# Moving two of three value loads to a second DMA queue in a decode-attention kernel

## The chip, the cores and the metric

One core of a Trainium2 chip. The metric is the device time of one execution in microseconds, the median of the runs. All runs told here are fast (none is over 1.5% above the fastest run of its kernel). Transfers are issued by an engine's sequencer into a queue (0.33 us an issue on SyncE); SyncE has one and ScalarE has one (q1 and q10 in the traces below), and the packets of both run on the core's 16 DMA engines. A load has landed when its completion is counted. A turn is three blocks, one for each buffer.

## The reference, cut to what matters

One query token attends to a cache of 65,536 keys and values in 16 heads of 256, beside a small dense branch:

```python
q = (xn @ wq).reshape(1, 1, 16, 256).transpose(0, 2, 1, 3)
scores = einsum("bhqd,bhkd->bhqk", q, k_cache) * 256 ** -0.5
o = einsum("bhqk,bhkd->bhqd", softmax(scores), v_cache)
out = x + (o.transpose(...).reshape(1, 1, 4096) @ wo) * silu(silu(xn @ w1) @ w2)
```

The cache is 1.07 GB and each byte is used once.

## The kernel before

The cache is cut into 64 blocks; a block's keys are one load of 128 partitions x 64 KB (8.389 MB), and so are its values. There are three buffers. In each, keys come in; VectorE forms the products with the query and sums them for 19 columns of 32, ScalarE sums the other 13; the values come into the same buffer; TensorE multiplies them with the exponentials; then the buffer takes the keys of three blocks later. SyncE issues everything:

```python
    def load_k(i, s, h=None):
        if h is not None:
            take(sp, h)                  # TensorE is past half of the buffer's values
        take(sp, vf[s])                  # TensorE is done with the buffer
        sp.dma_start(out=R[s][:, :], in_=block(Kd, i)).then_inc(kl[s], 16)
        ...
    def load_v(i, s):
        take(sp, kf[s])                  # VectorE's last copy of the block: keys are used up
        sp.dma_start(out=R[s][:, :], in_=block(Vd, i)).then_inc(vl[s], 16)
    ...
    def dve_block(s, between=None):      # VectorE, cut
        take(dve, qr)
        dve.tensor_copy(out=qcur[:, :], in_=ps_q).then_inc(sd, 1)
        take(dve, kl[s], 16)             # ALL of the block's keys must have landed
        ...                              # 4 x (one long multiply, 19 multiply-and-sum)
        take(dve, pf, 4)                 # ScalarE's last sums
        dve.tensor_copy(out=S2[...], in_=S[...]).then_inc(kf[s], 1)
        dve.reduce_max(out=rmax[:, :], in_=S[...], axis=AX.X).then_inc(rm, 1)
    ...
    def act_block(i, s):                 # ScalarE
        for k in range(NSTEP):
            if k == NSTEP // 2:
                act_keep(i - 2)
            act_sums(s, k)
        act_softmax(i, s)                # waits for the maximum, then the exponentials
    ...
        with nc.Fori(2 * NR, LAST - 2, NR, engines={ET.SP}, ...) as i:
            for s in range(NR):
                load_k(i + s, s, vh[s])
                load_v(i + s - 1, (s - 1) % NR)
```

The kernel waits until a load's counter has risen by 16, and the trace has 16 four-byte completion records to a load (112 for the seven loads in a window of 130 us). I take them as one for each engine (the records do not name theirs); so a load has landed when the slowest engine is done (in one block of before the last completion record came at 1222.0 and the landing was counted at 1222.46).

## Time and profile before

| | before |
|---|---|
| time, median of 3 runs (range) | 2520.83 us (2520.53 to 2522.59) |
| share of the span in which SyncE's DMA queue was busy | 99.7% |
| rate in steady slices | 433 GB/s |
| VectorE busy | 89% |
| VectorE's wait for keys | 190.1 us, 61 times |

The share of the queue says what bounds the kernel; VectorE's wait for keys says that the next in line has room. The lines themselves are shown, and read, in the prediction.

### The profile page before, as it was taken

Reading aid. Unit: us, or ns where it says so; the run is one execution under the profiler, and the core shown is the slowest. Engines: PE = TensorE matmul, PEld = TensorE weight load, DVE = VectorE, ACT = ScalarE, POOL = GpSimd, SP = SyncE. Lnnn points to the kernel's source line nnn. Section 1 sums busy time; section 2 is a strip of 40 time slices with the busy share of each in tenths; the row PEclk is TensorE's granted clock in tenths of the full one; section 3 lists DMA queues with packets and bytes.
Section 4 is the critical chain, followed back from the end, with each engine's and each line's share of the span. In section 5 each row is a group of like instructions: output and inputs, shape, how many; then the busy total and the mean of one; then the engine's idle time right before and its main releaser. Section 6 shows DMA issues by size and latency. Waiting matters only on the chain. (4 is left out here: it accounts for less than half of the span.)

```text
span 2518.0 us, 29489 instructions
## 1 busy us (share of the span) xinstructions
PE 1147.2 (46%) x4738; PEld 437.0 (17%) x4738; DVE 2233.4 (89%) x10277; ACT 1446.0 (57%) x6996; POOL 1.9 (0%) x14
## 2 busy tenths in 40 slices
PE   3253543534535435345354353453543534535457
PEld 1121211211112112112111121111111211211122
DVE  6979889889898898898998988989989889889897
ACT  4656556556565565565655655655556556556564
POOL 0000000000000000000000000000000000000000
PEclk7676766767667677677676776776776767767679
DMA  9999999999999999999999999999999999999998
GB/s 422 426 440 420 432 435 431 435 433 433 433 433 433 433 433 433 433 433 433 433 433 433 433 433 433 433 433 433 433 433 434 434 433 433 434 435 436 433 427 357
DMA packets 23316, 1084.47 MB, mean 431 GB/s; under 512 B 2434, under 2 KB 4612, under 8 KB 4996
## 3 DMA queue, kind: packets, MB, share of 16 engines
q1 hardware_dynamic: 23298, 1084.30, 99.7%
q8 instruction: 4, 0.07, 0.0%
q14 instruction: 12, 0.10, 0.0%
q10 hardware_dynamic: 2, 0.00, 0.0%
HBM read 1084.29 MB, written 0.00 MB: 431 GB/s over the span
## 5 line engine op out<-in xcount | busy, mean ns | idle before, releaser
L283 ACT ACTIVATE R<-R 128x256 bf16<-128x256 bf16 x3328 | 1330.8, 401 | 747.5 <-ACTq L159 747.5
L261 DVE CUSTOM_DVE_ANT_0 R<-R,qcur 128x256 bf16<-128x256 bf16 x4864 | 1700.3, 418 | 0.0
L330 PE MATMUL bank<-R,PV 128*2 128x512 bf16 x4096 | 1027.1, 417 | 29.6 <-DMA R<-in_A_v_cache_dram 11.5
L250 DVE TENSOR_TENSOR R<-R,qcur 128x3328 bf16<-128x3328 bf16 x256 | 482.8, 1886 | 190.1 <-DVEq L159 190.0
L283 ACT ACTIVATION_READ_ACCUMULATOR R<-R 128x1 f32 x3328 | 620.9, 187 | 0.0
L342 PE MATMUL bank<-ident,rmax 128*1 128x128 bf16 x65 | 17.1, 263 | 1076.8 <-PEq L159 1076.8
L330 PEld LDWEIGHTS bank<-R,PV 128*2 128x2 bf16 x4096 | 366.0, 90 | 662.4 <-issue 212.9
L261 DVE DVE_READ_ACCUMULATOR2_ANT S<- 128x1 f32 x4864 | 387.1, 80 | 0.0
L342 PEld LDWEIGHTS bank<-ident,rmax 128*1 128x1 bf16 x65 | 5.2, 79 | 1081.1 <-issue 1081.0
L359 PE MATMUL bank<-eye,O 2*128 2x2 f32 x264 | 40.0, 252 | 232.2 <-PEq L159 232.2
L296 ACT ACTIVATE hist<-bank 128x1 f32 (+1 forms) x65 | 11.1, 171 | 199.5 <-ACTq L159 199.5
L359 PEld LDWEIGHTS bank<-eye,O 2*128 2x128 f32 x264 | 36.2, 206 | 249.5 <-issue 249.5
L224 DVE TENSOR_REDUCE gmax<-bank 1x1 bf16<-1x128 f32 x65 | 18.3, 281 | 37.2 <-DVEq L159 37.2
L309 ACT COPY O<-bank 2x512 f32<-2x512 f32 x67 | 37.4, 559 | 21.6 <-ACTq L159 21.6
L317 ACT COPY hist<-bank 128x2 f32 (+1 forms) x66 | 10.5, 159 | 59.9 <-ACTq L159 59.9
L241 DVE CAST qcur<-bank 128x256 bf16<-128x256 f32 x64 | 27.2, 424 | 19.0 <-DVEq L159 19.0
L298 ACT ACTIVATE PV<-S,hist 128x128 bf16<-128x128 f32 (+1 forms) x65 | 26.0, 400 | 13.4 <-ACTq L159 13.1
L373 PE MATMUL bank<-q,ident 8*128 (+1 forms) x63 | 24.3, 386 | 7.7 <-issue 1.3
L234 DVE COPY S<-S 128x128 f32<-128x128 f32 (+1 forms) x65 | 14.7, 226 | 10.4 <-DVEq L159 1.1
L235 DVE TENSOR_REDUCE rmax<-S 128x1 bf16<-128x128 f32 (+1 forms) x65 | 18.1, 279 | 0.0
L348 PE MATMUL bank<-gmax,ones_row 1*128 1x1 bf16 x65 | 10.3, 159 | 4.5 <-PEq L159 0.6
L298 ACT ACTIVATION_READ_ACCUMULATOR PV<-S,hist (+1 forms) x65 | 12.1, 186 | 0.0
(68 smaller groups left out, 90.6 us busy)
## 6 DMA issues: line engine op xcount, KB each, us to landing
R<-in_A_k_cache_dram SPq DMA_DIRECT2D x7, 4096.0 KB, 27.3
R<-in_A_v_cache_dram SPq DMA_DIRECT2D x6, 2048.0 KB, 22.4
R<-in_A_k_cache_dram SPq DMA_DIRECT2D x2, 2048.0 KB, 20.1
R<-in_A_wq_dram SPq DMA_DIRECT2D x1, 3072.0 KB, 12.8
R<-in_A_v_cache_dram SPq DMA_DIRECT2D x3, 1024.0 KB, 25.0
R<-in_A_wo_dram SPq DMA_DIRECT2D x2, 1120.0 KB, 21.8
R<-in_B_w_dram SPq DMA_DIRECT2D x1, 1568.0 KB, 25.7
R<-in_B_w_dram SPq DMA_DIRECT2D x1, 1344.0 KB, 5.8
```

What stands on the lines that cost most here:

```text
L224: dve.reduce_max(out=gmax[0:1, :], in_=ps_m[0:1, :], axis=AX.X).then_inc(gm, 1)
L235: dve.reduce_max(out=rmax[:, :], in_=S[:, c0:c1], axis=AX.X).then_inc(rm, 1)
L241: dve.tensor_copy(out=qcur[:, :], in_=ps_q).then_inc(sd, 1)
L250: m = dve.tensor_tensor(out=pair, in0=pair, in1=qcur[:, None, :].to_broadcast([P, NA, Dh]), op=ALU.mult,)
L261: ins = dve.tensor_tensor_reduce(out=Kv[:, c, :], in0=Kv[:, c, :], in1=qcur[:, :], scale=1.0, scalar=0.0, op0=ALU.mult, op1=ALU.add, accum ...
L283: ins = act.activation(out=prod, in_=prod, func=ACT.Identity, accum_out=S[:, c : c + 1],)
L298: act.activation(out=PV[s][:, c0:c1], in_=S2[:, c0:c1], func=ACT.Exp, bias=col(0, 1), scale=scale, accum_out=col(1, 2),).then_inc(pv, 1)
L309: act.copy(out=O[:, :], in_=po).then_inc(oc, 1)
L330: ins = pe.matmul(po, lhsT=PV[t][:, c : c + 2], rhs=R[s][:, c * Dh : (c + 2) * Dh], start=(start and c == k0), stop=(stop and c == k1 - 2),)
L342: pe.matmul(ps_m[0:1, :], lhsT=rmax[:, 0:1], rhs=ident[:, :], start=True, stop=True).then_inc(tm, 1)
L359: ins = pe.matmul(ps_t2[:, 2 * a : 2 * a + 2], lhsT=Ov[:, j, a, :], rhs=eye2[:, j, :], start=(j == 0), stop=(j == 1), is_transpose=True,)
L373: pe.matmul(ps_q, lhsT=ident[0:HP, at(j)].to_broadcast([HP, P]), rhs=q8[:, o : o + Dh] if isinstance(o, int) else q8[:, bass.ds(o, Dh)], s ...
```

## The change

Its intent: take value loads out of SyncE's single stream of waits, so that one of them is issued as soon as ScalarE, which stands at the right place anyway, sees its condition met. The third buffer's value loads stay in SyncE's queue.

```diff
-    def load_v(i, s):
-        take(sp, kf[s])
-        sp.dma_start(out=R[s][:, :], in_=block(Vd, i)).then_inc(vl[s], 16)
+    def load_v(i, s, g=sp):
+        take(g, kf[s])
+        g.dma_start(out=R[s][:, :], in_=block(Vd, i)).then_inc(vl[s], 16)
@@ act_block
             act_sums(s, k)
+        if s < NR - 1:
+            load_v(i, s, act)
         act_softmax(i, s)
@@ SyncE's stream
         load_k(2, 2)
-        load_v(0, 0)
-        load_v(1, 1)
...
             load_k(NR + s, s, vh[s])
-            load_v(NR + s - 1, s - 1)
...
                 load_k(i + s, s, vh[s])
-                load_v(i + s - 1, (s - 1) % NR)
+                if s == 0:
+                    load_v(i - 1, NR - 1)
```

## The prediction

> **What bounds the kernel now.** I read the page's slices and queue table first, then the issues by line, then the timeline of SyncE, VectorE and TensorE in the middle of the run, and last the row that waits longest on the busiest engine.
>
> ```profile
> span 2518.0 us, 29489 instructions
> PE 1147.2 (46%) x4738; PEld 437.0 (17%) x4738; DVE 2233.4 (89%) x10277; ACT 1446.0 (57%) x6996; POOL 1.9 (0%) x14
> DMA  9999999999999999999999999999999999999998
> GB/s 422 426 440 420 432 435 431 435 433 433 433 433 433 433 433 433 433 433 433 433 433 433 433 433 433 433 433 433 433 433 434 434 433 433 434 435 436 433 427 357
> q1 hardware_dynamic: 23298, 1084.30, 99.7%
> L250 DVE TENSOR_TENSOR R<-R,qcur 128x3328 bf16<-128x3328 bf16 x256 | 482.8, 1886 | 190.1 <-DVEq L159 190.0
> ```
>
> The reader is to see that one DMA queue (SyncE's) is busy for 99.7% of the span and moves 433 GB/s slice after slice, while the busiest engine, VectorE, is at 89% and still waits 190 us. That wait is in 61 places, 3.1 us each: once in a block, for the block's keys. The transfers bound the kernel, and the VectorE is next. The chain of waits reaches back only to the last 7 us and says nothing of the loop.
>
> One block of the loop, from the timelines (start, duration, engine):
>
> ```profile
> 1218.00 0.33 SPq L207 DMA_DIRECT2D R<-in_A_v_cache_dram  x1
> 1236.26 0.33 SPq L201 DMA_DIRECT2D R<-in_A_k_cache_dram  x1
> 1256.70 0.33 SPq L207 DMA_DIRECT2D R<-in_A_v_cache_dram  x1
> 1274.39 0.33 SPq L201 DMA_DIRECT2D R<-in_A_k_cache_dram  x1
> 1295.50 0.33 SPq L207 DMA_DIRECT2D R<-in_A_v_cache_dram  x1
> 1312.52 0.33 SPq L201 DMA_DIRECT2D R<-in_A_k_cache_dram  x1
> ```
> ```profile
> 1217.61 0.23 DVE L234 COPY S<-S 128x128 f32<-128x128 f32 x1
> ...
> 1219.33 16.64 PE L330 MATMUL bank<-R,PV 128*2 128x512 bf16 x64
> 1219.40 0.17 ACT L296 ACTIVATE hist<-bank 128x1 f32 x1 [3.08 <-ACTq L159]
> ...
> 1222.60 1.89 DVE L250 TENSOR_TENSOR R<-R,qcur 128x3328 bf16<-128x3328 bf16 x1 [3.07 <-DVEq L159]
> ```
> ```profile
> R<-in_A_v_cache_dram SPq DMA_DIRECT2D x62, 23.8
> R<-in_A_k_cache_dram SPq DMA_DIRECT2D x60, 25.5
> ```
>
> A value load is issued 0.16 us after VectorE's copy ends (1217.84). A key load is issued when TensorE has used up a buffer: 17.0 to 18.3 us after the value load, 17.7 on average. Value issues stand 38.70 and 38.80 us apart; from 250.32 to 2417.77 they are 56 blocks, so a block takes 38.70 us and one load of 8.389 MB takes half, 19.35 us (433.5 GB/s). VectorE needs 34.1 us from the landing of its keys to the next value issue (1222.60 to 1256.70), then about 1.5 us for maximum and query before it could start again: 35.6 us, hence its 3.1 us of waiting. The value load of 1218.00 lands at 1241.8, but TensorE starts on it only after the next block's maximum, at 1258.03: values have 16 us to spare, keys none.
>
> [...]
> - [...] The trace of before can't show two queues side by side, but shows how little there is to save: 0.33 us an issue, on an engine that does nothing else.
> - [...]
> - [...]
> - [...] The trace: the 1344 KB load at the start lands 5.8 us after issue, of which 3.2 us is data at 433 GB/s, so 2.6 us; I use 2.6.
>
> **The change part by part.**
> 1. *Where the issue stands.* For two blocks of three, waiting for VectorE's copy and issuing the value load move to ScalarE. VectorE's copy itself waits for ScalarE's last sums, so ScalarE is there in time. It then waits anyway: 3.08 us idle before the bias copy that opens its exponentials, which started 1.56 us after the copy ended (1217.84 to 1219.40). The wake-up and issue, 0.16 + 0.33 us [...], fit in these 1.56 us. Cost on the path: 0. ScalarE gets 42 x 0.4 = 17 us more work, at 57% busy: 0.
> 2. *What SyncE loses.* 42 issues of 0.33 us and the fixed order of key and value loads. The issues alternate by themselves (value, 17.7 us, key, 21.0 us, value), and no load stood behind another's wait: each value issue follows the copy by 0.16 us. So nothing is issued earlier. Gain: 0.
> 3. *Bytes.* The same 1084.3 MB. [...] Gain: 0 to a few us.
> 4. *Order on the DMA engines, the one thing that changes.* [...] How much of the keys is left when a value load gets to the engines? The keys land 38.70 - 34.1 = 4.6 us after the value issue; less 2.6 fixed, about 2.0 us of data. Shared evenly, those 2.0 us take 4.0: the keys land 2.0 us later, VectorE starts 2.0 us later, and the next value load is issued 2.0 us later. Total work is the same, so the engines stay busy as long as some load is queued. Over three blocks: [...] the first from ScalarE delays its keys by 2.0; the second then comes 2.0 late, finds 2.0 - 2.0 = 0 left and delays nothing. VectorE's 3.1 us of slack absorbs the lateness before the next turn. So the queue runs just to zero once in three blocks: loss about 0, margin about 0. Key loads are safe: a key issue precedes the landing of the values by 5.5 us (1236.26 against 1241.8), 2.9 after the fixed part, 0.9 at 2.0 us of delay.
> 5. *Coarse packets.* Packets here are 64 KB (in a window of 130 us, 854 packets of 55.97 MB beside 112 tiny ones, 16 to a load), 8 per DMA engine and load, 19.35 / 8 = 2.4 us each. [...] a delay of 2.4 to 4.8 us in place of 2.0. Then the second ScalarE load comes 0.4 to 2.8 us after the queue ran dry. That is lost for good, once in three blocks, some 20 times: 8 to 56 us. Delays near 2.4 seem likelier than 4.8, [...] and I think even sharing or none at all as likely as both together.
> 6. *Start.* At the first value load (57.05) the second block's keys, and all of the third's, are still queued (landing 80.3 in before). Shared, the third block's keys land near 99.7, against VectorE ready at 94.2: 5.4 us late. Carried on through the next blocks, the queue has spare work until the fifth value load, which comes some 2 to 3 us after it ran dry. Loss: 3 us, once.
> 7. *Tail.* All its loads stay in SyncE's queue. 0.
>
> Sum: 2520.8 + 0 (issue) + 3 (start) + 0 to 56 for packets, weighted to about 5, and 0 for bytes: 2529 us.
>
> **The rivals.**
> (a) Nothing happens: completion comes before foreign packets, keys land as before, 2519 to 2523 us. For it: the slack of values, the same issue times, and the in-flight packet being most of the 2.0 us left.
> (b) [...] 2510 to 2515. Against it: 99.7% busy already.
> (c) The coarse packets delay keys by two packets each time, VectorE's slack is used up, and the DMA idles 2 to 3 us every third block: 2565 to 2580. For it: the margin is only 2.0 us and all 16 engines must be done before the keys count as landed; the slowest decides.
> (d) ScalarE's issue takes much longer than SyncE's, so that the exponentials and next sums are late. Against it: exponentials are needed only a block later, and ScalarE waits 747 us in front of its sums; up to 3 us an issue costs nothing.
>
> **Range and chances.** Rival (a) and even sharing together have about half of the weight (2519 to 2526), a loss of 0.4 to 1.5 us every third block some 35% (2530 to 2555), (c) about 8%, (b) 5%. That gives 2529 with 2515 to 2556 for 8 in 10. Faster by over 2% [...]: 0.01. Slower by over 2% needs 50 us, as in (c): 0.07. Within 2%: 0.92.
>
> **What would show it.** The queue table should show a second busy queue with 42 loads, 352 MB or about 32%, the share of both near 99%. Value loads from ScalarE should be issued at the same distance from VectorE's copy, ScalarE's idle before the bias copy stay near 3 us less the issue. The median landing of keys may rise by up to 2.4 us, of values to 24 to 28. VectorE's wait for keys keeps its sum (190 us) if the rate holds, and grows by exactly the time lost if not, with DMA share and GB/s of steady slices falling from 433 to 428 to 432. I am wrong if steady slices fall below 425, if ScalarE's sums come to hold up VectorE, or if key loads are issued later because values land late.

## The result, and the profile after

| | before | after |
|---|---|---|
| time, median of 4 runs (range) | 2520.68 us (2519.84 to 2522.59) | 2541.33 us (2539.67 to 2544.66) |
| ratio | | 1.0084 (95% interval 1.0070 to 1.0099) |

A ratio is the mean time of one kernel's fast runs over that of the other's in the same rounds, so it is not quite the ratio of the medians. Kernels are compared only within the same rounds. The changed kernel is slower by 0.8%, within 2%. All outputs are right. The profiled runs are 2518.0 us and 2542.9 us long, so 24.9 us are to be found.

The page of the changed kernel, its span, rate by slice, the two busy queues and VectorE's row that waits for keys (busy us, mean ns, then idle us and its releaser):

```profile
span 2542.9 us, 29537 instructions
GB/s 420 429 428 399 442 428 433 429 428 429 413 429 430 441 415 445 429 429 429 429 428 412 429 420 439 428 430 429 429 429 435 438 425 434 428 430 429 429 423 362
q1 hardware_dynamic: 17250, 731.98, 66.8%
q10 hardware_dynamic: 6050, 352.33, 32.6%
L250 DVE TENSOR_TENSOR R<-R,qcur 128x3328 bf16<-128x3328 bf16 x256 | 483.0, 1887 | 216.0 <-DVEq L159 215.8
```

The second queue carries 352 MB, nearly a third. The two shares still add up to 99.4%, and yet most slices move 428 to 430 GB/s in place of 433, and some much less. VectorE's wait for keys grew by 25.9 us, about what the span grew by. The same stretch of the loop in both kernels (columns: its bounds and length, busy time of PE, PEld, DVE, ACT and POOL, the granted TensorE clock, DMA share, GB/s); before:

```profile
450.00:2250.00 1800.00, 814.92 (x3371) 310.39 (x3368) 1616.37 (x7454) 1046.67 (x5080) 0.00 (x0) 0.71 1.00 434
```

and after:

```profile
450.00:2250.00 1800.00, 803.29 (x3320) 306.22 (x3321) 1597.91 (x7364) 1034.18 (x5017) 0.00 (x0) 0.70 1.00 429
```

A DMA share of 1.00 at 429 GB/s means that packets took longer, not only that engines stood idle. The busy shares of the engines say nothing about where; the order in time does. Three blocks of the changed kernel, from the timeline (start, duration, engine; in brackets what the engine waited just before; lines between are left out):

```profile
1229.09 0.23 DVE L234 COPY S<-S 128x128 f32<-128x128 f32 x1
1229.55 0.34 ACTq L207 DMA_DIRECT2D R<-in_A_v_cache_dram  x1
1230.88 0.17 ACT L296 ACTIVATE hist<-bank 128x1 f32 x1 [3.10 <-ACTq L159]
1236.46 1.89 DVE L250 TENSOR_TENSOR R<-R,qcur 128x3328 bf16<-128x3328 bf16 x1 [5.46 <-DVEq L159]
...
1270.64 0.34 ACTq L207 DMA_DIRECT2D R<-in_A_v_cache_dram  x1
1271.97 0.17 ACT L296 ACTIVATE hist<-bank 128x1 f32 x1 [3.08 <-ACTq L159]
1272.75 1.89 DVE L250 TENSOR_TENSOR R<-R,qcur 128x3328 bf16<-128x3328 bf16 x1 [0.65 <-DVEq L159]
...
1306.96 0.33 SPq L207 DMA_DIRECT2D R<-in_A_v_cache_dram  x1
...
1313.98 1.89 DVE L250 TENSOR_TENSOR R<-R,qcur 128x3328 bf16<-128x3328 bf16 x1 [5.42 <-DVEq L159]
```

Read the distance from a value issue to VectorE's next start, which is when the next keys have landed (0.14 us before the start). Before, it is 4.6 us for every load (1218.00 to 1222.60). Here it is 6.9 us after the first ScalarE load and 2.1 us after the second. The 7.0 us after SyncE's load are an exception with a cause of its own, told below; from SyncE's value issue to the keys' landing the median is 5.1 us. ScalarE itself lost nothing: its bias copy comes 1.56 us after VectorE's copy ends (1229.32 to 1230.88), the same as before.

What lies between is seen in the trace's records of single packets. A load is 128 packets of 64 KB, 2.42 us each, and 16 4-byte completion records: eight packets and one record for each DMA engine. The records do not name their engine, so I took a record that starts where another ends as the next one of the same engine. This is one of the 16 at each of two loads (issued at 1112.86 and 1153.98; K are packets of keys, V of values, K+ the keys' completion):

```
first ScalarE load                          second ScalarE load
K 1113.85-1116.28                           K  1152.62-1155.04
V 1116.27-1118.69  (issued at 1112.86)      K+ 1155.04
K+ 1118.69                                  V  1155.04-1158.09  (issued at 1153.98; 3.05 us)
V 1118.70-1121.11                           V  1158.09-1160.51
keys counted as landed: 1119.66             keys counted as landed: 1155.94
```

At this first load, 13 of the 16 engines served one packet of values between the last packet of keys and the keys' completion. Over the 16 turns from block 9 it was 1 to 14 engines, and one is enough to delay the landing (in the three turns with one, the last completion record came 2.4 to 2.9 us after the last of the keys' data). The keys' data were complete on every engine by 1116.9 and were counted as landed 2.8 us later (2.5 to 3.3 us over these turns). In the one queue of before, this gap is 0.5 us (last completion record 1222.0, landing 1222.46). VectorE starts 2.3 us late, so the second value load is issued 2.3 us late, reaches the engines when they are finishing their last packet, and its first packet starts with a gap or takes about 3 us in place of 2.42. I added up these gaps and overlong packets near each value issue, as a mean over the 16 engines and over blocks 9 to 57:

| lost per value load, us | first of three | second | third |
|---|---|---|---|
| before | 0.04 | 0.01 | 0.01 |
| after | 0.17 | 0.98 | 0.01 |

That is 1.16 us a turn of three blocks; over the 18 turns from block 5 to block 59 it makes 20.9 us, and those turns together grew by 21.9 us (2090.15 to 2112.04, between VectorE's copies of the two blocks). Fifteen of these turns took 116.3 to 117.5 us, three took 119.5 to 119.8; before, every one took 116.1 to 116.2.

Another 2.0 us are lost before block 5. VectorE's start and the fifth value load in the changed kernel:

```profile
182.39 1.89 DVE L250 TENSOR_TENSOR R<-R,qcur 128x3328 bf16<-128x3328 bf16 x1 [10.96 <-DVEq L159]
216.58 0.34 ACTq L207 DMA_DIRECT2D R<-in_A_v_cache_dram  x1
218.14 1.89 DVE L250 TENSOR_TENSOR R<-R,qcur 128x3328 bf16<-128x3328 bf16 x1
```

VectorE did not wait before the start at 218.14: the keys (landed at 216.36) were there before the value load was even issued, and nothing else was queued. Before, the fifth value load was issued at 211.34 and keys landed 4.6 us after it. The packet records show fewer than half of the engines busy for 4.1 us here. The rest, about 1 us, is after block 59.

### The profile page after: what moved, and what is told of

Read it like the earlier page. It is cut to its first block, busy times and chain, and to the rows that moved or that the text cites.

```text
span 2542.9 us, 29537 instructions
## 1 busy us (share of the span) xinstructions
PE 1142.4 (45%) x4738; PEld 436.5 (17%) x4738; DVE 2233.5 (88%) x10277; ACT 1446.9 (57%) x6996; POOL 1.9 (0%) x14
## 3 DMA queue, kind: packets, MB, share of 16 engines
q10 hardware_dynamic: 6050, 352.33, 32.6%
```

## The experiments

**Theory T**: with two queues, the completion of the keys stands behind a packet of values; VectorE is late, the next value load is late and finds too little queued; the DMA engines lose time at its first packet. **Rival R1**: ScalarE's waiting or issuing at this place costs. **Rival R2**: each entry into a second queue has a price of its own, whoever comes late.

| run | median us | ratio to before | keys land after the three value issues of a turn, us |
|---|---|---|---|
| before | 2520.3 to 2520.7 | 1 | 4.5, 4.5, 4.4 |
| after | 2541.33 | 1.0084 | 6.8, 2.0, 5.1 |
| relay, one queue | 2520.89 | 1.0004 | 4.3, 4.3, 4.3 |
| one of three | 2538.74 | 1.0076 | 6.8, 2.0, 5.0 |
| all three | 2582.00 | 1.0251 | 7.1 to 9.2 and 2.0 in turn |
| after, halved values | 2540.55 | 1.0099 | 5.7, 3.2, 4.8 |
| before, halved values | 2525.25 | 1.0019 | 4.5, 4.5, 4.4 |
| after, shorter VectorE | 2540.14 | 1.0086 | 7.6, 2.8, 5.5 |
| before, shorter VectorE | 2519.70 | 0.9997 | 5.3, 5.3, 5.2 |
| after, small first DMA | 2564.93 | 1.0184 | 4.8, 5.8, 5.2 |
| before, small first DMA | 2524.66 | 1.0016 | 4.5, 4.5, 4.4 |
| late, spoilt | 2622.39 | 1.0404 | 6.4, 3.1, 6.3 |
| late by 2.4 us, one queue | 2533.94 | 1.0071 | 4.5, 2.1, 4.8 |
| late by 1.2 us, one queue | 2538.85 | 1.0071 | 4.5, 3.4, 5.4 |

The last column has medians over the value loads issued between 400 and 2300 us of each profiled run; for all three, the range of most loads. Where a load is cut, its first DMA counts.

### Relay: ScalarE's place without its queue

```diff
-        take(sp, kf[s])
+        take(sp, af[s] if s < NR - 1 else kf[s])
         sp.dma_start(out=R[s][:, :], in_=block(Vd, i)).then_inc(vl[s], 16)
@@ act_block of the kernel before
+        if s < NR - 1:
+            take(act, kf[s])
+            act.sem_inc(af[s], 1)
         act_softmax(i, s)
```

> ScalarE waits for VectorE's copy at the place of the change and passes a signal on; SyncE, which waits for that signal, issues all value loads in its own queue. Theory T (with two queues the completion of the keys waits behind one 64 KB packet of the values, VectorE and the next value load come 2.3 us late and the DMA engines run dry): the place costs nothing, 2519 to 2524 us. Rival R1 (it is ScalarE's waiting or issuing at this place that costs): 2533 to 2541 us.

Measured: 2520.89 us. One block, from the timeline:

```profile
1219.15 0.23 DVE L235 COPY S<-S 128x128 f32<-128x128 f32 x1
1219.66 0.33 SPq L208 DMA_DIRECT2D R<-in_A_v_cache_dram  x1
1224.13 1.89 DVE L251 TENSOR_TENSOR R<-R,qcur 128x3328 bf16<-128x3328 bf16 x1 [3.06 <-DVEq L159]
```

The value load is issued 0.12 us later after the copy than in before, and nothing follows from it. ScalarE's wait at this place is free. The relay doesn't let ScalarE issue a load; that part of R1 is answered by the trace of the changed kernel, where an issue took 0.34 us and the bias copy came as soon after VectorE's copy as before (1.56 us). What is left is the queue.

### One of three

```diff
@@ act_block
+        if s == 0:
+            load_v(i, s, act)
@@ SyncE's stream: load_v(0, 0) goes, and in the loop
-                load_v(i + s - 1, (s - 1) % NR)
+                if s != 1:
+                    load_v(i + s - 1, (s - 1) % NR)
```

> Only the value loads of the first buffer are issued from ScalarE; those of the other two stay in SyncE's queue. T: the keys that follow a ScalarE load land 6.8 us after its issue (4.5 without it), so the next value load, which is now SyncE's, is the late one, with keys landing only 2.0 us after it; the loss stays one late load in three, 0.6 to 0.8 us a turn of three blocks, and the time is 2530 to 2540 us. Rival R2 (each entry into the second queue has a price, about 0.5 us, whoever comes late): half of the loss, about 2531 us, and the SyncE load after it as punctual as in before (4.4 us).

(The lines of SyncE's stream are shown against the kernel before.) Measured: 2538.74 us. Two value issues and VectorE's starts after them:

```profile
1227.62 0.34 ACTq L207 DMA_DIRECT2D R<-in_A_v_cache_dram  x1
...
1234.54 1.89 DVE L250 TENSOR_TENSOR R<-R,qcur 128x3328 bf16<-128x3328 bf16 x1 [5.47 <-DVEq L159]
...
1268.66 0.33 SPq L207 DMA_DIRECT2D R<-in_A_v_cache_dram  x1
...
1270.83 1.89 DVE L250 TENSOR_TENSOR R<-R,qcur 128x3328 bf16<-128x3328 bf16 x1 [0.64 <-DVEq L159]
```

This settles T against R2 more clearly than the time does. The load that is late is now one of SyncE's own queue (2.2 us from issue to VectorE's start). In the packet records the loss is at this load, 0.58 us, and the ScalarE load, the only one that enters a second queue, loses 0.03 us. An entry in good time costs almost nothing by itself; what it does is to delay the keys. The median lies inside T's range, near its upper end; the four runs spread from 2535.7 to 2541.5.

### All three

```diff
@@ act_block; SyncE's value loads of the loop go
-        if s < NR - 1:
+        if s < NR - 1 or not (isinstance(i, int) and i == LAST - 1):
             load_v(i, s, act)
@@ the last three blocks are written out, so that the last one can leave its load to SyncE
-        loop(act, 0, LAST, NR, act_block, slot=128)
+        loop(act, 0, LAST - NR, NR, act_block, slot=128)
+        for s in range(NR):
+            act_block(LAST - NR + s, s)
```

> All value loads of the loop are issued from ScalarE. T: late and punctual loads alternate (keys land 6.8 and 2.0 us after the value issue), a pattern of two blocks in place of three, some 30 late loads in place of 20: 2540 to 2556 us. R2: 63 entries in place of 42, each alike: about 2552 us without a pattern of two.

Measured: 2582.00 us, with the expected pattern of two (keys 2.0 us after one value issue, and 7.1 to 9.2 us after the next). The size was missed by both theories. Here keys land up to 2.4 us later still than in the changed kernel, and the engines stood idle for 34 us in the loop against 8 in the changed kernel (packet records, 260 to 2380 us). So the third load in SyncE's own queue, after which keys land at 5.1 us in place of 4.4 before, is what keeps the change from costing 2.5%. Why the keys land later still here was not tried.

### Halved values, after and before

```diff
-        g.dma_start(out=R[s][:, :], in_=block(Vd, i)).then_inc(vl[s], 16)
+        for w in (slice(0, KW // 2), slice(KW // 2, KW)):
+            g.dma_start(out=R[s][:, w], in_=block(Vd, i)[:, w]).then_inc(vl[s], 16)
@@ pe_v
-        take(pe, vl[s], 16)
+        take(pe, vl[s], 32)
```

> The changed kernel with each value load of the loop cut into two DMAs of half the columns, so that its packets are 32 KB and take 1.2 us. T: the completion of the keys waits behind a 1.2 us packet in place of a 2.4 us one, so keys land 5.6 us after the ScalarE issue, the next value load comes 1.2 us late with 3.2 us left, [...] and the engines do not run dry: 2520 to 2529 us. R2: no gain, 2540 us or more with twice the number of issues.

> Control: the kernel before with the value loads cut in the same way, all in SyncE's queue. Both theories: 2518 to 2524 us, keys landing 4.4 us after each value issue.

Measured: 2540.55 us after, 2525.25 us before (the cut alone costs 5 us). The mechanism scales as T says: with packets of half the size keys land 1.2 to 1.3 us later than before in place of 2.3, and the second load's distance is 3.2 us in place of 2.0. The time does not follow, a miss for T: 15 us over its control in place of 21, with R2's range (2540 us or more) met. That 3.2 us would be enough was my estimate, and it was wrong: they are still too few.

### Shorter VectorE, after and before

```diff
-ND = 19
+ND = 18
```

> The changed kernel with one column of 32 moved from VectorE to ScalarE, which shortens VectorE's block by about 0.8 us (4 x (0.345 - 0.145)) and so issues each value load 0.8 us earlier. T: the late load has 2.0 + 0.8 = 2.8 us left, [...] so most of the loss goes: 2522 to 2531 us. R2: the loss stays, 2538 to 2543 us.

> Control: the kernel before with the same column moved. Both theories: the transfers bound it, 2518 to 2523 us; keys land 5.2 us after each value issue and VectorE waits 3.9 us a block.

Measured: 2540.14 us after (2533.8 to 2546.2), 2519.70 us before. A miss for T, in the same way, and within R2's range (2538 to 2543). The margin grew by 0.8 us as worked out, and the second load now comes with 2.8 us left, but in the profiled run (one of 2533.8 us) it still lost 0.49 us on average. The wide spread of the two-queue kernel has no counterpart in its control (2519.3 to 2519.9).

### Late by 2.4 us in one queue, first try

Seven multiply-and-sum instructions on a query row, in front of every third block of VectorE, in the kernel before.

> The kernel before, all loads in SyncE's queue, but in every third block VectorE first does seven products of a query row with itself (7 x 0.345 = 2.4 us), so that this block's value load comes as late as the second ScalarE load of the changed kernel does. T: lateness alone makes the DMA engines run dry, in whatever queue: keys land 2.0 us after the late value issue, a turn of three blocks takes 0.5 to 0.8 us more, 2529 to 2537 us. R2 (two queues as such have the price): VectorE's 3.1 us of slack hides it, 2519 to 2523 us.

Measured: 2622.39 us, and not a test of anything asked. With its 14 more instructions in VectorE's loop, the instruction queue moved 74 packets in the 1800 us from 450 to 2250 where before it moved none in the loop, and VectorE stood 5.4 us before a query copy that otherwise waits 0.3 us. With the count of instructions restored (the mended runs below) the queue moves 12 packets in the whole run, as before. The run is set aside.

### A small first DMA, after and before

As in the halved kernels, cut at 16 of 128 columns in place of 64.

> The changed kernel with each value load of the loop cut into a first DMA of 16 of 128 columns (packets of 8 KB, 0.3 us) and a second of the rest. T: the keys' completion waits only behind an 8 KB packet, keys land 4.8 to 5.2 us after the ScalarE issue, no load comes late: at most 6 us over the same cut in one queue. R2: 12 to 20 us over it.

> Control: the kernel before with the same cut, all in SyncE's queue. Both theories: 2520 to 2527 us (the same cut in halves took 2525), keys landing 4.4 us after the value issue.

Measured: 2564.93 us after, 2524.66 us before. The keys that follow the first ScalarE load were nearly on time, as T expected (4.8 us), and yet this is the worst but two of the kernels, 40 us over its control: a miss for T, and more than R2's 12 to 20 us. In the packet records the loss has moved: at ScalarE's loads the first packet of the second, larger DMA starts late (about 12 us of gaps in the loop, a mean over engines), and packets of that DMA are slow (some 20 us in all, 15 of them in the first packets, against 2 in its control's). So a cheap completion for the keys is not enough, and this cut opens a new seam inside the value load. Why these packets are slow is not settled.

### Late by 2.4 and by 1.2 us in one queue, mended

```diff
@@ dve_block of the kernel before
         take(dve, kl[s], 16)
+        if s == 1:
+            dve.tensor_reduce(out=spare[:, :], in_=ones_sq[:, None, :].to_broadcast([P, 17, P]),
+                              axis=AX.X, op=ALU.max)
...
-            if k == 1:
+            if k == 1 and s != 1:
                 take(dve, kq[s], 16)
```

The second kernel has 8 in place of 17. The wait that goes out, with its increments in SyncE's stream, is always met for this buffer, so the count of instructions stays the same.

> The last late run was spoilt: its 14 more instructions a loop made VectorE fetch its program again in each turn. Here the delay is a single maximum over 17 copies of a constant row (about 2.4 us) in every third block, and a wait that is always met goes out in its place. All loads in SyncE's queue. T: the value load of that block finds keys landing 2.0 us after it, as the second ScalarE load does, and its first packets are late and slow: 0.5 to 0.8 us a turn, 2529 to 2537 us. R2 (the price is that of two queues): 2519 to 2523 us.

> The same with 8 copies (about 1.2 us): keys land 3.2 us after the value issue. T: between none and half of the other run's loss, 2521 to 2529 us; it shows from which lead on a load is punctual. R2: 2519 to 2523 us.

Measured: 2533.94 us and 2538.85 us. Two blocks of the first (the instruction queue is back at 12 packets in all):

```profile
1224.68 0.33 SPq L209 DMA_DIRECT2D R<-in_A_v_cache_dram  x1
1229.28 2.42 DVE L247 TENSOR_REDUCE spare<-ones_sq 128x17 f32<-128x2176 f32 x1 [3.05 <-DVEq L160]
1231.61 1.88 DVE L259 TENSOR_TENSOR R<-R,qcur 128x3328 bf16<-128x3328 bf16 x1
...
1265.72 0.33 SPq L209 DMA_DIRECT2D R<-in_A_v_cache_dram  x1
1268.05 1.89 DVE L259 TENSOR_TENSOR R<-R,qcur 128x3328 bf16<-128x3328 bf16 x1 [0.81 <-DVEq L160]
```

Keys landed punctually at 1229.1, VectorE began 2.3 us later, and the next value load had 2.3 us to VectorE's start, as the second ScalarE load of the changed kernel has. There is one queue only, VectorE's slack is not used up (it still waits 0.81 us afterwards), and the kernel is 13.6 us slower than before (2533.94 - 2520.3). Lateness by itself costs, in the old queue too; R2 as the whole cause is out. The loss per load is 0.43 us at the late one and 0.04 us at the one before it, against 0.98 and 0.17 in the changed kernel. By the medians, lateness of 2.4 us in one queue costs 13.6 us and the change 20.7.

The packet records also show how lateness costs, and that it does so nearly alike with one queue and with two. In none of the ten traces with uncut value loads did a value load of blocks 9 to 57 start its first packet on an engine less than 0.95 us after its issue, or end it less than 3.86 us after. The sooner an engine comes to the load, the longer is this packet (means, against 2.42 us):

| first packet starts after the issue | changed kernel | one of three | late by 2.4 us, one queue |
|---|---|---|---|
| 0.9 to 1.2 us | 3.13 us long | 3.13 | 3.11 |
| 1.2 to 1.5 us | 2.95 | 2.90 | 2.84 |
| 1.5 to 1.8 us | 2.81 | 2.74 | 2.68 |

So a load loses time on every engine that comes to it less than about 1.5 us after its issue (3.86 - 2.42 = 1.44, an estimate from these figures), though the engine never runs dry. What the changed kernel loses beyond this is mostly idle time: its engines stood idle for 0.39 us at a late load, on average, and for 0.03 us in this kernel.

Where does the rest come from? In the changed kernel's turns that were long (119.5 us and more), single engines had fallen a packet behind the others. One of them began its first packet of the value load of 1270.64 1.2 to 2.0 us after the rest, and took 3.58 us for it; in the next keys it was still behind, and these landed 6.9 us after the value issue of 1306.96 in place of 5.1. A load has landed when the slowest engine is done, so one laggard makes VectorE late. That the second queue brings such laggards is not shown. The changed kernel has 3 of 18 turns over 119 us and the one-queue kernel late by 2.4 us none; but one of three, with two queues, has none either (at most 118.1 us). The profiles are also unlike: the changed kernel's is of the slowest of its four runs, the one-queue kernel's of the fastest of its four, which reach up to 2546.5 us. What decides when a laggard arises was not tried.

The 1.2 us delay was expected to cost less than the 2.4 us one, and cost no less: a miss for T, whose range ended at 2529. It lost 0.77 us at the late load and 0.48 at the one before it, as much a turn as the changed kernel (1.25 against 1.16), in one queue; by the medians it costs 18.6 us. Its slowest engine lost about 2.5 us on average where the median engine lost less than 0.5; with 2.4 us of delay it was 0.7 and 0.4. So the engines come apart in one queue, too. Why they do so more at the smaller delay stays open, and with it what share of the changed kernel's loss the second queue has beyond making the load late.

## Why the prediction was right

The median, 2541.3, lies in the range of 2515 to 2556, 12 us above the 2529 that was named, and within 2% was given 0.92. The range held because step 5 had put the delay of a packet into it; that the time fell inside so well owes something to luck, as half of the weight lay on no loss in the loop.

- **What bounds the kernel, steps 1, 2, 3 and 7** held. The queues together stayed at 99.4%; 42 issues moved with 352.33 MB; ScalarE's idle time before its bias copy stayed at 3.1 us; the relay showed that the place costs nothing; the tail added about 1 us where 0 was said. Step 3's gain of up to a few us, and with it the 2510 to 2515 us of rival (b), was my estimate; no run shows such a gain. One reading was loose: VectorE's copy is followed by the value issue after 0.16 us in two blocks of three and after 0.25 us in the third, not by 0.16 us each time; nothing hangs on it.
- **Step 4, the order on the DMA engines,** had the pattern right: the first ScalarE load delays its keys (2.0 us predicted, 2.3 measured), the second comes late, VectorE's slack takes it up before the load in SyncE's queue. Its reason, even sharing, was wrong: the keys' data were hardly delayed (complete 4.0 us after the first ScalarE issue, the median of the 17 turns from block 9, and in before their last completion record came 4.0 us after the value issue, too). It is the completion record that stands behind one packet: the last one came at 6.4 us, 2.4 us after the data. Step 5 had the delay of a packet, as a possibility. And step 4's "loss about 0, margin about 0" was wrong: the second load, like each load in these runs that was issued only 2.0 to 3.4 us before the keys landed, lost time at its first packet before the queue was empty (0.98 us here).
- **Step 5** was the right term and mis-sized: "weighted to about 5" us for the loop, where the profiled run lost 21.9. In its own words, 0.4 to 2.8 us once in three blocks: measured 0.98 + 0.17 us. The delay is of one packet, as it thought likelier, but its reason for the loss, that the load comes 0.4 to 2.8 us after the queue ran dry, did not hold: the load was issued 2.0 us before the keys landed. By its sum a delay of one packet would have cost only 0.4 us. The weight that I gave to "even sharing or none at all" should have gone to the packet.
- **Step 6, the start,** held: the third block's keys were to land near 99.7 and landed at 99.75; the queue was to run dry at the fifth value load, and did; 3 us were predicted, 2.0 were lost by block 5.
- **Of the rivals,** (a) would have kept the keys' landing, which moved by 2.3 us; (b), a faster loop, did not happen, its rate fell from 434 to 429 GB/s; (c)'s delay by up to two packets shows only with all three loads on ScalarE (keys up to 9.2 us after the value issue in place of 4.5), at 2582 us; (d) fell with ScalarE's issue of 0.34 us and its bias copy at the same 1.56 us.
- **Signs.** VectorE's wait for keys was to grow by the time lost: it grew by 25.9 us, the span by 24.9. Key loads were issued no later than before (17.5 us after the value load, on average, against 17.7). Steady slices were to read 428 to 432: most read 428 to 430, and the stretch from 450 to 2250 reads 429. Single slices did fall below 425 (412 to 420 in the loop), which I had called a refutation; they are the slices of the long turns and of loads whose bytes are counted in the next slice, and I should have named a mean.

None of the 13 other kernels was faster than the one before beyond the noise; the nearest, the shorter VectorE in one queue, stands at 0.9997 (0.9981 to 1.0014).

## What to carry to other kernels

Here, where transfers bound the kernel, a second queue on the same DMA engines added no bandwidth (429 against 434 GB/s in the loop), and it put another load's packet in front of the completion record of the load that an engine was waiting for (counted as landed 2.8 us after its last data, in place of 0.5). Look for the load that is needed the moment it lands, and keep what can overtake it in the same queue (the relay, with all loads in one, had the keys 4.3 us after the value issue and took 2520.89 us). Where the DMA is the bound, the margin to watch is how much is still queued when the next load is issued: here 4.4 us kept it fed as long as the engines were abreast (0.48 us were lost at such a load where they were not), while 2.0 to 3.4 us, though not zero, already cost about half a microsecond or more each time, in one queue as in two.
